# Routing search by counting: threshold masks as matmul weights and the experts' one-hot columns moving, in an attention, MoE and capacity-routing kernel

## The chip, the cores and the metric

The kernel runs on one core of one Trainium2 chip. The metric is the device time of one execution in microseconds (us); lower is better. Three runs of the kernel before took 1225.27, 1225.92 and 1227.36 us, the median is 1225.92 us.

## The reference, cut to what matters

Three stages, each feeding the next. The change touches mainly the third, the search for the routing's thresholds.

```python
# 1 attention of x (8,8,512,64) and state (8,8,32,64), both ways, concatenated: 8 x 544 tokens of 512
# 2 dense MoE on the tokens
h = x @ w_in                                            # 512 -> 2048
g = np.maximum(h, 0.0) + np.log1p(np.exp(-np.abs(h)))   # softplus
x = g @ w_out                                           # 2048 -> 512
# 3 routing with a capacity
N, E = x.shape[0], 8
cap = N // E
logits = x @ w_gate
for idx in np.argsort(-logits.flatten()):               # best pair first
    tok, e = idx // E, idx % E
    if assigned[tok] >= 0 or counts[e] >= cap:
        continue
    assigned[tok] = e
    counts[e] += 1
for e in range(E):
    mask = assigned == e
    out[mask] = np.maximum(x[mask] @ w1[e], 0.0) @ w2[e]
```

The program has 8 x 544 = 4352 tokens, and a capacity of 544 per expert.

## The kernel before, in words

**Stages.** Attention and the dense MoE are interleaved over eight batches of 544 tokens (`attention`, generator in batches 1 to 7, beside `mlp1`, the product with w_in at L485, the softplus at L520 to L550, and `mlp2`, the product with w_out at L569 to L580). Each fp32 operand is split in a high and a low part, and each product is three matmuls. The softplus is four steps: ACT copies p_h out (L520), takes an exponential and a logarithm (L527, L528, the helper `softplus_log`, one call of which does both for a pending tile), and DVE adds them up to g (L540). ACT then writes g_hi (L548), POOL the difference g_lo (L551). L540 also frees the PSUM bank of p_h, of which there are few, so that PE's next L485 waits for it. In `attention`, DVE scales and transposes Z into `back` (L290, L291), ACT copies that to at_hi (L292), and POOL takes at_lo.

**The routing.** The greedy loop of the reference is done in eight phases; each fills one expert. A phase finds, for all eight experts at once, the value v at which an expert becomes full, as the bits of a float, in seven steps (five bits in the first four, four bits in the last three: 31, 31, 31, 31, 15, 15 thresholds and 16, with one more column in the last). Tokens lie on 128 partitions by NJ = 34 columns, padded to NJ4 = 36. A step is:
- mask, L1015 on DVE: mk[token, threshold] = v >= threshold;
- count, L912 (`by_some`) on PE: the one-hot of each token's expert is the weight, the masks move, and the counts come out with a row per expert. `by_some` takes 2 columns of tokens per matmul in phase 0 (17 matmuls) and 4 in phases 1 to 6 (9 matmuls), each for another diagonal block of the result;
- sum of the blocks and comparison with the places that are left, L1036 to L1039 on DVE (8 rows of 31): pe, then sat;
- L1046 on PE: a matmul with ones brings the number of full experts of each threshold to all partitions;
- L1049 on DVE: d, df, the digit found, from which the next thresholds come (L1010).

After step 7 the phase ends with a tail: ohd, junk, cnt, s (L1054 to L1059) on 8 rows, T (L1062), one bf16 matmul that brings s to all partitions, gt, tie, cg, asg (L1065 to L1068), ec, em, ei (L1071 to L1073: which expert is filled), M (L1075, L1076), the matmul of M (L919), positions (L921 to L943), the matmuls with R (L912), the index list and a gather of the expert's tokens (xg).

**What sets the order.** `route` is a generator: at each `wait` it hands control back, and the code around it emits so many matmuls of the main work in between. Phase 0 runs between the last `mlp2` matmuls (717.9 to 756.6 us; fillers of 0.233 us each by a table BETWEEN), phases 1 to 6 between the expert matmuls (757 to 1061 us, slots AT1, AT2, AT3), one phase beside the previous expert; phase 7 has nothing to search. PE runs in program order, so a count whose mask isn't there yet stops the main work too; DVE, ACT, POOL and SP also run in program order. `route_consts` makes the search's constants, at step s == NFT + 4 of `mlp1` (DVE, 175.0 to 178.3 us). `y_state` writes the state tokens' result, four DMAs of 32 rows in each of two parts (L634), on the queues of SP and ACT in turn.

Of the kernel before, what the change touches and what calls it, by code (L numbers as in the profile page):

```python
# [22 lines left out]
NJ = N // 128  # L23
# [7 lines left out]
def attn_moe_kernel(ctx, tc, x_s, x_t, state_t, w_in, w_out, w_gate, w1, w2, out):  # L31
# [46 lines left out]
    iof = const.tile([8, 16], F32, name="iof")  # L78
    tri = const.tile([128, 128], BF, name="tri")
    code = const.tile([128, E], F32, name="code")  # L80
    code8 = const.tile([E, 1], F32, name="code8")
# [170 lines left out]
    def attention(b):  # L252
# [31 lines left out]
        for par in range(2):  # L284
# [6 lines left out]
            V.transpose(back[:, par], Z[:, par])  # L291
            A.activation(hi[:, par], back[:, par], AF.Copy)  # L292
# [368 lines left out]
    def first_step(j0, j1):  # L661
# [131 lines left out]
    for s in range(NX - 2):  # L793
        b, ft = divmod(s, NFT)
        if s == NX - NFT:
# [82 lines left out]
    iof_t, pel_t, rem8_t = small(1 << BITS[-1]), small((1 << BITS[-1]) + 1), small(1)  # L878
# [81 lines left out]
    def route(ph, slow=True):  # L960
# [31 lines left out]
        for s, bits in enumerate(BITS):  # L992
# [5 lines left out]
            if s or ph:  # L998
                mk = rt.tile([128, NJ, n + (2 if last else 0)], BF, name="mk", tag=f"mk{n}_{last}")
# [25 lines left out]
            ps = [p[0:E] for p in by_some(bg(), om, mk, w, 4 if slow else 2)]  # L1025
            sat = sats[n]
            pe = rt.tile([E, w], F32, name="pe", tag=f"pe{w}")
            if last:
                V.tensor_copy(pe, ps[0])
                for p in ps[1:-1]:  # L1030
                    V.tensor_tensor(pe, p, pe, op=OP.add)
                V.tensor_tensor(pel, ps[-1], pe, op=OP.add)
                pe = pel
                V.tensor_scalar(sat[0:E], pe[:, 1:1 + n], rem8, None, op0=OP.is_ge)
# [36 lines left out]
        V.tensor_tensor(ec, p[:, 0:E], code, op=OP.mult)  # L1071
# [300 lines left out]
```

## Time and profile before

| what | value |
|---|---|
| median of 3 runs | 1225.92 us |
| the profiled execution's own time | 1226.8 us |
| its span, first to last instruction | 1225.0 us |
| granted TensorE clock, mean | 0.990 |
| PE busy | 1159.3 us, 95% |
| DVE, ACT, POOL busy | 667.3, 639.2, 487.8 us |
| phase 0 of the search | 717.9 to 756.6 us |
| phases 1 to 6 | 770 to 1061 us |

The profile is of one execution. Its own time is 1.8 us more than its span, and 0.9 us more than the median of the runs. A row of the timeline is: start, duration, engine and line, operation, output<-inputs, shapes, count, and in brackets how long the engine sat idle before it and for whom. Matmuls are pipelined: the durations of neighbours overlap, and the distance from start to start is what one costs.

### The profile page before, as it was taken

The numbers are of one execution on the slowest core, as the hardware profiler recorded it, in microseconds if no ns is written. First come the engines' busy times: TensorE is split into PE (matmuls) and PEld (weight loads), VectorE is DVE, ScalarE is ACT, GpSimd is POOL, SyncE is SP. The second block draws the span as 40 slices with busy tenths as digits, with TensorE's granted clock in tenths as the row PEclk, the third lists the DMA queues.
The fourth block names the chain that finished last, engine by engine and source line by source line (L and its number), as shares of the span: only waits on it lengthen the run. The fifth ranks groups of instructions, "written<-read, shape, count | busy, mean of one in ns | idle before, by whom it ended". The sixth has DMA issues, their size and how long they took to land.

```text
span 1225.0 us, 21305 instructions
## 1 busy us (share of the span) xinstructions
PE 1159.3 (95%) x8291; PEld 910.3 (74%) x8291; DVE 667.3 (54%) x1797; ACT 639.2 (52%) x1277; POOL 487.8 (40%) x466
## 2 busy tenths in 40 slices
PE   4898999999999999999999997999999999999996
PEld 1565676777677776777677765879797988789895
DVE  6998545353363543634434266777685868751120
ACT  3776656666666666666666732533343333333330
POOL 0334323222232232222344425645647555546531
PEclk9998999999999999999999998999999999999999
DMA  7463021111201112002000003251523415234200
GB/s 241 139 202 127 1 70 35 53 52 36 69 1 52 52 35 58 13 36 69 1 18 18 1 18 123 88 194 40 180 92 129 150 68 172 104 108 140 89 18 37
DMA packets 51061, 95.78 MB, mean 78 GB/s; under 512 B 4624, under 2 KB 19088, under 8 KB 50960
## 3 DMA queue, kind: packets, MB, share of 16 engines
q1 hardware_dynamic: 45136, 76.33, 18.8%
q0 software_dynamic: 5632, 17.83, 4.2%
q8 instruction: 65, 1.06, 0.4%
q10 hardware_dynamic: 192, 0.26, 0.1%
q14 instruction: 36, 0.29, 0.1%
HBM read 76.58 MB, written 17.83 MB: 77 GB/s over the span
## 4 chain that ended last, share of the span: by engine, by line
PE 66%; DVE 17%; ACT 7%; issue 6%; POOL 2%; DMA 1%; SPq 0%; ACTq 0%; POOLq 0%; DVEq 0%
PE p_y L1310 12%; PE p_h L485 10%; PE p_y L1265 6%; PE p_y L569 6%; PE p_y L571 5%; PE p_h L1265 5%; PE p_y L573 5%; PE p_bg L912 2%; DVE g L540 2%; PE p_y L576 2%; PE p_bg L454 2%; PE p_bg L496 2%; PE p_y L578 2%; PE p_y L580 2%; PE p_h L1176 1%
## 5 line engine op out<-in xcount | busy, mean ns | idle before, releaser
L551 POOL TENSOR_TENSOR g_lo<-g,g_hi 128x512 fp32r<-128x512 f32 x127 | 164.9, 1299 | 340.7 <-ACT g_hi L548 327.3
L569 PE MATMUL p_y<-g_hi,wo_hi 128*128 128x512 f32 x448 | 185.0, 413 | 0.0
L571 PE MATMUL p_y<-g_hi,wo_lo 128*128 128x512 f32 x448 | 177.7, 397 | 3.7 <-POOL wo_lo L232 3.7
L573 PE MATMUL p_y<-g_lo,wo_hi 128*128 128x512 f32 x448 | 177.2, 396 | 0.0
L540 DVE SCALAR_TENSOR_TENSOR g<-p_h,t_sp 128x512 f32<-128x512 f32 x128 | 87.7, 686 | 122.7 <-ACT t_sp L528 121.8
L548 ACT ACTIVATE g_hi<-g 128x512 fp32r<-128x512 f32 x126 | 79.6, 632 | 124.0 <-DVE g L540 95.2
L569 PEld LDWEIGHTS p_y<-g_hi,wo_hi 128*128 128x128 f32 x448 | 85.1, 190 | 48.3 <-issue 15.9
L485 PE MATMUL p_h<-at_hi,P_hi 128*128 128x512 f32 x256 | 104.9, 410 | 8.1 <-DVE g L540 8.1
L1310 PE MATMUL p_y<-w2h,h2h 128*128 128x512 f32 x256 | 105.1, 411 | 0.0
L485 PE MATMUL p_h<-at_hi,P_lo 128*128 128x512 f32 x256 | 101.8, 398 | 0.0
L485 PE MATMUL p_h<-at_lo,P_hi 128*128 128x512 f32 x256 | 101.7, 397 | 0.0
L1310 PE MATMUL p_y<-w2l,h2h 128*128 128x512 f32 x256 | 101.5, 396 | 0.0
L1310 PE MATMUL p_y<-w2h,h2l 128*128 128x512 f32 x256 | 101.3, 396 | 0.0
L571 PEld LDWEIGHTS p_y<-g_hi,wo_lo 128*128 128x128 f32 x448 | 85.4, 191 | 21.0 <-POOL wo_lo L232 4.9
L573 PEld LDWEIGHTS p_y<-g_lo,wo_hi 128*128 128x128 f32 x448 | 85.2, 190 | 21.0 <-POOL g_lo L551 2.4
L1318 POOL DMA_INDIRECT out_dram<-ot,idx x40 | 39.4, 985 | 145.6 <-ACT ot L1316 68.9
L1149 POOL TENSOR_TENSOR w2l<-s2w,w2h 128x512 fp32r<-128x512 f32 x64 | 82.5, 1305 | 14.2 <-ACT w2h L1148 13.0
L520 ACT ACTIVATE t_sp<-p_h 128x512 f32<-128x512 f32 x128 | 75.3, 588 | 24.5 <-PE p_h L485 24.2
L1149 POOL TENSOR_TENSOR w1l<-s1w,w1h 128x512 fp32r<-128x512 f32 x63 | 80.4, 1300 | 11.2 <-ACT w1h L1148 10.3
L528 ACT ACTIVATE t_sp<-t_sp 128x512 f32<-128x512 f32 x128 | 80.9, 632 | 4.1
L527 ACT ACTIVATE t_sp<-t_sp 128x512 f32<-128x512 f32 x128 | 80.6, 630 | 2.0
L1265 PE MATMUL p_y<-yTh,w1h 128*128 128x288 f32 (+1 forms) x256 | 76.9, 300 | 0.6 <-DVE h2t L1274 0.6
(284 smaller groups left out, 2643.5 us busy)
## 6 DMA issues: line engine op xcount, KB each, us to landing
s1w<-in_moe_w_dram SPq DMA_DIRECT2D x8, 2048.0 KB, 8.4
s2w<-in_moe_w_dram SPq DMA_DIRECT2D x8, 2048.0 KB, 9.5
st<-in_moe_w_in_dram SPq DMA_DIRECT2D x16, 512.0 KB, 4.1
xT<-in_x_t_dram SPq DMA_DIRECT2D x16, 512.0 KB, 4.4
st<-in_moe_w_out_dram SPq DMA_DIRECT2D x16, 512.0 KB, 3.7
xt<-in_x_s_dram SPq DMA_DIRECT2D x8, 1024.0 KB, 5.8
y_d<-yz SPq DMA_DIRECT2D x48, 128.0 KB, 3.6
y_d<-s_g SPq DMA_DIRECT2D x8, 128.0 KB, 2.2
```

Of the source, the lines that this page charges most:

```text
L485: PE.matmul(h, l[:, f0:f0 + 128], r[:, par, :], start=(n == 0), stop=(n == 5))
L527: A.activation(t, t, AF.Exp, scale=-1.0)
L528: A.activation(t, t, AF.Ln, bias=1.0)
L540: V.scalar_tensor_tensor(g[:, :w], hps.pop(s)[:, :w], 0.0, tsp.pop(s)[:, :w], op0=OP.max, op1=OP.add)
L548: A.activation(hi[:, c], g[:, c], AF.Copy)
L551: (G if on[1] == "G" else V).tensor_tensor(lo[:, c], g[:, c], hi[:, c].bitcast(F32), op=OP.subtract)
L569: PE.matmul(yb[j], wo_hi[:, ft, c], hi, start=st, stop=False)
L571: PE.matmul(yb[j], wo_lo[:, ft, c], hi, start=False, stop=False)
L573: PE.matmul(yb[j], wo_hi[:, ft, c], lo, start=False, stop=sp)
L1149: eng.tensor_tensor(lo, src, hi.bitcast(F32), op=OP.subtract)
L1265: PE.matmul(p[:, :w], l[:, k, f], r[:, k, c], start=(n == 0), stop=(n == 11))
L1310: PE.matmul(p, l[:, ft, c], r[:, ft, :], start=(n == 0), stop=(n == 23))
```

## The change

- **Counting.** The mask tiles are now 32 wide per token column, zeroed once (`mks`, `first[3]`), of which 31, 15 or 17 are written. They are the weights (4 columns of tokens, 128 x 128), and the one-hot (now 8 wide, `ohu`) moves with 32 columns: 9 matmuls a step in every phase. Counts have a row per threshold and a column per expert.
- **The rest of the search in that layout.** pe and sat are [thresholds, 8]; each step adds four blocks, in phase 0 too, where there were two. L1046 becomes a matmul of a constant 128 x 128 (`taken`) with sat, 8 columns; df is one TENSOR_REDUCE.
- **The tail.** ohd, junk and cnt go; oh2 is one operation. T is two fp32 matmuls with 128 x 128 weights (oh2 spread out) and pel moving. s8 and rem8 are read from its result, and stand ahead of gt, tie, cg and asg.
- **Constants.** `route_consts` loses five small operations, and two of the memsets, and gains 20 (row23, and six for each of three `taken`).
- **Beside it.** `attention` calls `softplus_log()` ahead of the at_hi copy; `y_state` sends the first part's four DMAs from SP.

```diff
+        for n, t in taken.items():
+            k0, k1 = (1, 15) if n == 16 else (0, n - 1)
+            rows = tp.tile([128, 2], F32, name=f"rows{n}")
+            V.tensor_scalar(rows[:, 0:1], pf, float(k0), None, op0=OP.is_ge)
+            V.tensor_scalar(rows[:, 1:2], pf, float(k1), None, op0=OP.is_le)
+            V.tensor_tensor(rows[:, 0:1], rows[:, 0:1], rows[:, 1:2], op=OP.mult)
+            V.tensor_scalar(rows[:, 1:2], pf, 32.0, float(1 << 23), op0=OP.is_equal, op1=OP.mult)
+            V.tensor_tensor(rows[:, 0:1], rows[:, 0:1], rows[:, 1:2], op=OP.add)
+            V.tensor_copy(t, bc(rows[:, 0:1], [128, 128]))
...
             V.transpose(back[:, par], Z[:, par])
+            softplus_log()
             A.activation(hi[:, par], back[:, par], AF.Copy)
...
-            (SP if i % 2 else A).dma_start(y_d[r0:r0 + NS], t[i * NS:(i + 1) * NS, 0])
+            (A if j and i % 2 else SP).dma_start(y_d[r0:r0 + NS], t[i * NS:(i + 1) * NS, 0])
...
-                V.tensor_tensor(mk[:, :, 0:w], bc(v[:, :, None], [128, NJ, w]), bc(tf[:, None, :], [128, NJ, w]),
+                V.tensor_tensor(mk[:, 0:NJ, 0:w], bc(v[:, :, None], [128, NJ, w]), bc(tf[:, None, :], [128, NJ, w]),
                                 op=OP.is_ge)
...
-            ps = [p[0:E] for p in by_some(bg(), om, mk, w, 4 if slow else 2)]
+            p = bg()
+            for j in range(0, NJ4, 4):
+                PE.matmul(p[:, 0:4 * E], mk[:, j:j + 4].rearrange("p a b -> p (a b)"),
+                          om[:, j:j + 4].rearrange("p a b -> p (a b)"), start=(j == 0), stop=(j + 4 >= NJ4))
+            ps = [p[q * 32:q * 32 + w, q * E:(q + 1) * E] for q in range(4)]
...
-                V.tensor_scalar(pe, ps[-1], -1.0, rem8, op0=OP.mult, op1=OP.add)
+                V.scalar_tensor_tensor(pe, ps[3], -1.0, rem8[0:w], op0=OP.mult, op1=OP.add)
                 for p in ps[1:-1]:
                     V.scalar_tensor_tensor(pe, p, -1.0, pe, op0=OP.mult, op1=OP.add)
-                V.tensor_tensor(sat[0:E], ps[0], pe, op=OP.is_ge)
+                V.tensor_tensor(sat[0:w], ps[0], pe, op=OP.is_ge)
...
-            PE.matmul(q[:, 0:n], ones_b, sat, start=True, stop=True)
-            d16 = rt.tile([128, n], F32, name="d16", tag=f"d{n}")
+            PE.matmul(q[:, 0:E], taken[16 if last else n], sat, start=True, stop=True)
             df = rt.tile([128, 1], F32, name="df")
-            V.scalar_tensor_tensor(d16, q[:, 0:n], 0.5, one23[:, 0:n], op0=OP.is_ge, op1=OP.add, accum_out=df)
+            V.tensor_reduce(df, q[:, 0:E], axis=AX, op=OP.max)
...
-        ohd = rt.tile([E, n + 1], F32, name="ohd")
-        V.tensor_scalar(ohd, iof_t[:, 0:n + 1], df[0:E], None, op0=OP.is_equal)
-        cnt = rt.tile([E, 2], F32, name="cnt")
-        junk = rt.tile([E, n + 1], F32, name="junk")
-        for i in range(2):
-            V.scalar_tensor_tensor(junk, pe[:, i:i + n + 1], 1.0, ohd, op0=OP.mult, op1=OP.mult, accum_out=cnt[:, i:i + 1])
-        V.tensor_tensor(s8[0:E], cnt[:, 0:1], rem8, op=OP.is_ge)
+        oh2 = rt.tile([128, 2], F32, name="oh2")
+        V.tensor_scalar(oh2, row23p, df, None, op0=OP.is_equal)
         yield from wait(WT, slow)
         p = bg()
-        PE.matmul(p[:, 0:E], bc(s8, [128, 128]), i8b, start=True, stop=True)
-        V.tensor_tensor(rem8, rem8, cnt[:, 1:2], op=OP.subtract)
+        for i in range(2):
+            PE.matmul(p[:, i * E:(i + 1) * E], bc(oh2[:, i:i + 1], [128, 128]), pel, start=True, stop=True)
+        V.tensor_tensor(s8, p[:, 0:E], rem8, op=OP.is_ge)
+        V.tensor_tensor(rem8, rem8, p[:, E:2 * E], op=OP.subtract)
         tf = fb.bitcast(F32)
...
-        V.tensor_tensor(ec, p[:, 0:E], code, op=OP.mult)
+        V.tensor_tensor(ec, s8, code, op=OP.mult)
```

How this moves instructions, at three places. Line numbers of the changed program are higher by 5 to 13 from L110 on. The first is ACT in the middle of an attention batch of the program before (at_hi is the copy of the transposed attention, t_sp the pending softplus):

```order
L548 ACTIVATE g_hi<-g 128x512
L520 ACTIVATE t_sp<-p_h 128x512
L292 ACTIVATE at_hi<-back 128x512
L527 ACTIVATE t_sp<-t_sp 128x512
L528 ACTIVATE t_sp<-t_sp 128x512
```

and of the changed program:

```order
L554 ACTIVATE g_hi<-g 128x512
L526 ACTIVATE t_sp<-p_h 128x512
L533 ACTIVATE t_sp<-t_sp 128x512
L534 ACTIVATE t_sp<-t_sp 128x512
L298 ACTIVATE at_hi<-back 128x512
```

The exponential and the logarithm now stand ahead of the copy that waits for DVE's transpose; so at 12 places.

The second is DVE at the tail of phase 0, from the digit of the last step on (L1049, now L1065). T, the matmul, lies between s (L1059) and ec (L1071) before; in the changed program it lies between oh2 (L1070) and L1075 (s8):

```order
L1054 TENSOR_SCALAR ohd<-p_bg_6872,df 8x16
L1058 SCALAR_TENSOR_TENSOR junk,cnt<-p_bg_6872,ohd 8x16 x2
L1059 TENSOR_TENSOR s_6886<-cnt,p_bg_6872 8x1
L1063 TENSOR_TENSOR p_bg_6872<-p_bg_6872,cnt 8x1
L1065 TENSOR_SCALAR p_bg_6872<-v_5974,p_bg_6872 128x34
L1066 TENSOR_SCALAR p_bg_6872<-v_5974,p_bg_6872 128x34
L1067 TENSOR_TENSOR p_bg_6872<-cu_5975,p_bg_6872 128x34
L1068 TENSOR_TENSOR asg<-asg,p_bg_6872 128x34
L1071 TENSOR_TENSOR ec<-p_bg_7334,code 128x8
```

```order
L1070 TENSOR_SCALAR oh_7278<-p_bg_6890,df 128x2
L1075 TENSOR_TENSOR p_bg_6890<-p_bg_7302,rem_6895 128x8
L1076 TENSOR_TENSOR rem_6895<-rem_6895,p_bg_7302 128x8
L1078 TENSOR_SCALAR p_bg_6890<-v_5991,p_bg_6890 128x34
L1079 TENSOR_SCALAR p_bg_6890<-v_5991,p_bg_6890 128x34
L1080 TENSOR_TENSOR p_bg_6890<-cu_5992,p_bg_6890 128x34
L1081 TENSOR_TENSOR asg<-asg,p_bg_6890 128x34
L1084 TENSOR_TENSOR ec<-p_bg_6890,code 128x8
```

Before, the four operations on 34 columns stood ahead of the first reader of T's result; now they stand behind it.

The third is PE at the first count of phase 0. In the changed program (before: 17 pairs of `LDWEIGHTS ohu` and `MATMUL p_bg<-mk,ohu 64x62`):

```order
L582 MATMUL p_y_6041<-wo_hi,g_hi 128x512
L1041 LDWEIGHTS mk_5994
L1041 MATMUL p_bg_6934<-ohu_5993,mk_5994 128x32
L1041 LDWEIGHTS mk_5994
L1041 MATMUL p_bg_6934<-ohu_5993,mk_5994 128x32
```

Nine such pairs take the place of 17; the main work around them stands as before.

## Rows read from the trace of the kernel before

**Rows 1.** One of PE's waits: us in total, times, longest.

```profile
PE p_h L485 <- DVE g L540: 8.1, 12, 1.4
```

**Rows 2.** Timeline of PE, DVE and ACT at the attention copy of one batch.

```profile
279.33 0.39 PE L573 MATMUL p_y<-g_lo,wo_hi 128*128 128x512 f32 x1
280.57 0.50 PE L485 MATMUL p_h<-at_hi,P_hi 128*128 128x512 f32 x1 [0.85 <-DVE g L540]
...
279.82 0.69 DVE L540 SCALAR_TENSOR_TENSOR g<-p_h,t_sp 128x512 f32<-128x512 f32 x1 [1.95 <-ACT t_sp L528]
...
277.90 0.63 ACT L292 ACTIVATE at_hi<-back 128x512 fp32r<-128x512 f32 x1 [3.05 <-DVE back L291]
```

**Rows 3.** Timeline of PE and ACT at the first part of `y_state`.

```profile
745.16 0.49 PE L576 MATMUL p_y<-wo_hi,g_hi 128*128 128x512 f32 x1 [1.36 <-ACT g_hi L548]
...
744.79 0.51 ACT L548 ACTIVATE g_hi<-s_g 128x128 fp32r<-128x128 f32 x2 [3.06 <-DVE yt L631]
```

**Rows 4.** Timeline of PE at a count of phase 0, with the fillers around it.

```profile
717.57 0.40 PE L576 MATMUL p_y<-wo_hi,g_hi 128*128 128x512 f32 x1
717.89 0.72 PE L912 MATMUL p_bg<-mk,ohu 128*64 128x62 bf16 x17
...
718.88 0.40 PE L580 MATMUL p_y<-wo_hi,g_lo 128*128 128x512 f32 x1
```

**Rows 5.** Timeline of PE at a count over 31 thresholds of phase 1.

```profile
776.16 0.28 PE L1265 MATMUL p_h<-yTh,w1h 128*128 128x256 f32 x1
776.27 0.64 PE L912 MATMUL p_bg<-mk,ohu 128*128 128x124 bf16 x9
...
776.95 0.28 PE L1265 MATMUL p_h<-yTh,w1l 128*128 128x256 f32 x1
777.07 0.28 PE L1265 MATMUL p_h<-yTh,w1h 128*128 128x256 f32 x1
```

**Rows 6.** Timeline of PE at a count over 15 thresholds of phase 1.

```profile
787.57 0.29 PE L1265 MATMUL p_h<-yTh,w1h 128*128 128x288 f32 x1
787.71 0.42 PE L912 MATMUL p_bg<-mk,ohu 128*128 128x60 bf16 x9
...
788.19 0.29 PE L1265 MATMUL p_h<-yTh,w1l 128*128 128x288 f32 x1
788.32 0.29 PE L1265 MATMUL p_h<-yTh,w1h 128*128 128x288 f32 x1
```

**Rows 7.** Timeline of PE at four fp32 transposes with 128 x 128 weights.

```profile
778.98 0.60 PE L1176 MATMUL p_h<-ident,xg 128*128 128x128 f32 x4
```

**Rows 8.** Groups of DVE's instructions, 757 to 1084 us: busy us, mean ns, idle before.

```profile
L1015 DVE TENSOR_TENSOR mk<-v,p_bg 128x1054 bf16<-128x1054 f32 x18 | 22.5, 1252 | 0.6
L1038 DVE SCALAR_TENSOR_TENSOR pe<-p_bg,pe 8x31 f32<-8x31 f32 x48 | 8.8, 182 | 1.7
L1066 DVE TENSOR_SCALAR p_bg<-v,p_bg 128x34 f32<-128x34 f32 x6 | 1.6, 260 | 0.2
```

**Rows 9.** DVE's line for R, ns min/median/max; it writes 17 of every 34 elements.

```profile
L943 DVE TENSOR_TENSOR R<-a,dig x16: 747/759/3747, 754.8 to 1082.8; 128x578 bf16<-128x578 f32 x16
```

**Rows 10.** Timeline at the end of `route_consts`: DVE, then PE.

```profile
177.02 0.29 DVE L116 TENSOR_SCALAR tri<-io,pf 128x128 bf16<-128x128 int32 x1
177.59 0.16 DVE L121 TENSOR_SCALAR rid<-pq 128x1 int32<-128x1 int32 x1
178.33 0.68 DVE L540 SCALAR_TENSOR_TENSOR g<-p_h,t_sp 128x512 f32<-128x512 f32 x1
...
180.08 0.40 PE L485 MATMUL p_h<-at_hi,P_hi 128*128 128x512 f32 x1
```

**Rows 11.** Timeline at the tail of phase 0: T, the first reader of T, the matmul of M.

```profile
748.18 0.18 PE L1062 MATMUL p_bg<-i8b,s 128*128 128x8 bf16 x1
749.45 0.16 PE L919 MATMUL p_bg<-ones_b,M 128*68 128x1 bf16 x1
...
748.42 0.17 DVE L1071 TENSOR_TENSOR ec<-p_bg,code 128x8 f32<-128x8 f32 x1 [0.17 <-PE p_bg L1062]
```

More of the change, by code (lines that the diff above doesn't have):

```diff
@@ L77, in attn_moe_kernel @@
     io = const.tile([128, 128], I32, name="io")
-    iof = const.tile([8, 16], F32, name="iof")
+    row23 = const.tile([128, 2], F32, name="row23")
+    taken = {n: const.tile([128, 128], BF, name=f"taken{n}") for n in (31, 15, 16)}
     tri = const.tile([128, 128], BF, name="tri")
     code = const.tile([128, E], F32, name="code")
-    code8 = const.tile([E, 1], F32, name="code8")
     pat = const.tile([128, sum((1 << b) - 1 for b in BITS) + 1], I32, name="pat")
@@ L84, in attn_moe_kernel @@
     ones_b = const.tile([128, 128], BF, name="ones_b")
-    one23 = const.tile([128, 31], F32, name="one23")
-    i8b = const.tile([128, E], BF, name="i8b")
     dig = const.tile([128, 2, NJ], F32, name="dig")
@@ L112, in route_consts @@
         V.memset(ones_b, 1.0)
-        V.tensor_copy(i8b, ident[:, 0:8])
         pf = tp.tile([128, 1], F32, name="pf")
         V.tensor_copy(pf, pcol)
+        for i in range(2):
+            V.tensor_scalar(row23[:, i:i + 1], pf, float((1 << 23) - i), None, op0=OP.add)
+        for n, t in taken.items():
[7 more added lines that the diff above has]
+            V.tensor_copy(t, bc(rows[:, 0:1], [128, 128]))
         V.tensor_scalar(tri, io, pf, None, op0=OP.is_gt)
@@ L803, in attn_moe_kernel @@
             first += [sp_.tile([128, NJ], F32, name="v0"), sp_.tile([128, NJ], F32, name="cu0"),
-                      sp_.tile([128, NJ4, 32], BF, name="ohu0"), sp_.tile([128, NJ, (1 << BITS[0]) - 1], BF, name="mk0")]
+                      sp_.tile([128, NJ4, E], BF, name="ohu0"), sp_.tile([128, NJ4, 32], BF, name="mk0")]
             G.memset(first[2], 0.0)
+            G.memset(first[3], 0.0)
         if s == NFT:
@@ L877, in attn_moe_kernel @@
     est = small(E)
-    iof_t, pel_t, rem8_t = small(1 << BITS[-1]), small((1 << BITS[-1]) + 1), small(1)
     sl, sh = small(NJ, sci), small(NJ, sci)
@@ L881, in attn_moe_kernel @@
     thr_t, patfb_t = small(31, sci), small(31, sci)
-    iof_t, pel, rem8 = iof_t[0:E], pel_t[0:E], rem8_t[0:E]
-    V.tensor_copy(iof_t, iof)
+    s8, row23p = small(E), small(2)
+    V.tensor_copy(row23p, row23)
     V.memset(U, 1.0)
@@ L886, in attn_moe_kernel @@
     V.memset(asg, 0.0)
+    rem8 = rt.tile([128, E], F32, name="rem8")
     V.memset(rem8, float(CAP))
+    pel = rt.tile([128, E], F32, name="pel")
+    V.memset(pel, 0.0)
     opn = rt.tile([128, E], F32, name="opn")
     V.memset(opn, 1.0)
-    ohu = rt.tile([128, NJ4, 32], BF, name="ohu")
+    ohu = rt.tile([128, NJ4, E], BF, name="ohu")
     G.memset(ohu, 0.0)
+    mks = {n: rt.tile([128, NJ4, 32], BF, name=f"mk{n}") for n in (31, 15)}
     ohl = rt.tile([128, NJ4, 32], BF, name="ohl")
     G.memset(ohl[:, NJ:], 0.0)
-    sats = {n: rt.tile([128, n], BF, name=f"sat{n}") for n in sorted({(1 << b) - 1 for b in BITS})}
-    s8 = rt.tile([128, 1], BF, name="s8")
-    for t in (*sats.values(), s8):
+    sats = {n: rt.tile([128, E], BF, name=f"sat{n}") for n in (31, 15, 16)}
+    for t in sats.values():
+        G.memset(t, 0.0)
+        G.memset(t[32:33], 1.0)
+    for t in mks.values():
         G.memset(t, 0.0)
@@ L998, in route @@
             if s or ph:
-                mk = rt.tile([128, NJ, n + (2 if last else 0)], BF, name="mk", tag=f"mk{n}_{last}")
+                mk = mks[n]
             if s == 0:
@@ L1024, in route @@
             yield from wait(W31 if n > 15 else W15, slow)
-            ps = [p[0:E] for p in by_some(bg(), om, mk, w, 4 if slow else 2)]
-            sat = sats[n]
-            pe = rt.tile([E, w], F32, name="pe", tag=f"pe{w}")
+            p = bg()
[3 more added lines that the diff above has]
+            ps = [p[q * 32:q * 32 + w, q * E:(q + 1) * E] for q in range(4)]
+            sat = sats[16 if last else n]
+            pe = rt.tile([w, E], F32, name="pe", tag=f"pe{w}")
             if last:
                 V.tensor_copy(pe, ps[0])
[L1030 to L1034, printed above, removed]
+                V.tensor_tensor(pe, ps[1], pe, op=OP.add)
+                V.tensor_tensor(pe, ps[2], pe, op=OP.add)
+                V.tensor_tensor(pel[0:w], ps[3], pe, op=OP.add)
+                V.tensor_tensor(sat[0:w], pel[0:w], rem8[0:w], op=OP.is_ge)
             else:
-                V.tensor_scalar(pe, ps[-1], -1.0, rem8, op0=OP.mult, op1=OP.add)
+                V.scalar_tensor_tensor(pe, ps[3], -1.0, rem8[0:w], op0=OP.mult, op1=OP.add)
                 for p in ps[1:-1]:
                     V.scalar_tensor_tensor(pe, p, -1.0, pe, op0=OP.mult, op1=OP.add)
-                V.tensor_tensor(sat[0:E], ps[0], pe, op=OP.is_ge)
+                V.tensor_tensor(sat[0:w], ps[0], pe, op=OP.is_ge)
             if 0 < s and not last:
@@ L1081, in route @@
         V.scalar_tensor_tensor(U, v, tf, U, op0=OP.is_le, op1=OP.mult)
-        e8 = rt.tile([E, 1], F32, name="e8")
-        V.tensor_scalar(e8, code8, em[0:E], 1.0e6, op0=OP.is_equal, op1=OP.mult)
-        V.tensor_tensor(rem8, rem8, e8, op=OP.add)
         V.tensor_scalar(est, code, em, None, op0=OP.is_equal)
+        V.scalar_tensor_tensor(rem8, est, 1.0e6, rem8, op0=OP.mult, op1=OP.add)
         V.tensor_tensor(opn, opn, est, op=OP.subtract)
```

12 lines of the change are left out of this document (4 added, 8 removed).

## The prediction, made before the changed kernel had run

> **What bounds the kernel now.** I read the page's busy times first: PE is busy for 1159.3 of the 1225.0 us of the span, so what PE issues less, or waits less, is time won, and a faster DVE or ACT is worth something only where PE waits for it. Next PE's list of waits. One entry belongs to a place that the change touches: L485 waits 12 times, 8.1 us in all, for DVE's g [rows 1]. The timeline at one such place [rows 2] shows why: the copy at_hi sat at the head of ACT's queue for 3.05 us, waiting for DVE's transpose, and the exponential and the logarithm of a tile long there stood behind it; g waited 1.95 us for them, and PE for g. Third, the timeline at `y_state`: ACT waited 3.06 us for DVE's yt, because two DMAs that read yt stood in its queue, and PE waited 1.36 us for the g_hi behind them [rows 3]. Last, the counts. They aren't waits but work on PE, and their price is what they push the next fillers back.
>
> All sums are against the profiled execution, 1226.8 us by its own time; the median of the runs is 0.9 us lower, and the number at the end stands against the median.
>
> **Attention, -8.4 us.** Moved ahead of at_hi, the logarithms run in the time in which ACT idled. g can then follow the transpose on DVE at 277.87, when at_hi began [rows 2], in place of 279.82, 1.95 us earlier, and PE had lost only about 1.0 us. The wait is gone with 0.9 us to spare. Of the 12 waits one (the longest, 1.4 us, in the first batch, before this loop) stays; 11 go, 8.1 - 1.4 = 6.7 us by the modelled ends. From start to start it is more: 280.57 - 279.33 = 1.24 us, less the usual pitch of 0.233, is 1.01 where the wait reads 0.85, so 0.16 more each, 11 x 0.16 = 1.8. Together 8.4. What is late next: at_hi itself, 1.2 us later behind both logarithms only where the transposes come early, and no PE row waits for it. Bounds: -8.4 and -4 (half comes back as a wait for the same g behind DVE's transposes).
>
> **`y_state`, -1.5 us.** 1.36 by the row, plus the same 0.16 [rows 3]. SP issues four DMAs in place of two; nothing stood near it on SP there, so I cost that at nothing. What covers it is that SP's next job, a weight load, stands well behind; without that cover this load would start later by the issue of two DMAs.
>
> **The count on PE, -8.5 us.** Price of a chain: from the filler ahead of it to one behind, less the pitch of the fillers. In phase 0, 718.88 - 717.57 less two of 0.233 is 0.84 us [rows 4]. Over 31 thresholds in phases 1 to 6, 777.07 - 776.16 less three of 0.12 is 0.55 [rows 5]; over 15, 788.32 - 787.57 less three of 0.133 is 0.35 [rows 6]. The new chain is nine matmuls with 32 columns and 128 x 128 weights, which the trace doesn't have. Upper bound: the nine of 60 columns, 0.35. Lower bound: 124 to 60 columns saved 0.20, so another 28 fewer could save 0.09, 0.26. I take 0.35, because the floor seems reached: the chains of phase 0 cost 0.05 a matmul at half the columns of the 124. That gives 7 x (0.84 - 0.35) = 3.4 in phase 0, 24 x 0.20 = 4.8 for 31 thresholds, nothing for 12 chains of 15, and 6 x 0.05 for those of 17 (an estimate between the two rows): -8.5. With 0.26, 49 x 0.09 = 4.4 more.
>
> The Trainium skill's page "TensorE: Matmul & The Clock Gate", section "Wait — 56ns, not 53.3ns?", puts a floor of about 25 ns under the distance of two matmuls however few their columns. By it nine would go from 0.35 to some 0.31 us at best, and the sum would be 2 us lower; rows 6, at 0.35 for nine, agree that little is left.
>
> **T, +1.4 us.** One bf16 matmul becomes two in fp32 with weights that must be loaded. The nearest row is four fp32 matmuls in 0.60 us [rows 7], so two are 0.30, against 0.18 for T now [rows 11]. Bounds +0.1 and +0.4 each; I take 0.2, times 7.
>
> **DVE between count and sat, +1.5 us.** Phase 0 adds two operations a step, 0.18 and a gap of some 0.04 each [rows 8], 0.43 us; the reduce in place of d and its accumulator gives back about 0.2, but behind the other matmul. Phase 0's fillers between count and L1046 are as few as three, 0.7 us, and the count itself is 0.49 shorter, so PE comes sooner to a sat that is later. Where three to six fillers stand between, I get waits of 0.2 to 0.7 us in four steps, 1.5 in all. Bounds 0 and 3. Phases 1 to 6 had four blocks already; there I put 0.8 for waits at counts that are first in a phase, where the load of the mask as weight can't run ahead of the mask. Bounds 0 and 2.
>
> **The tail, +2.4 us.** Before, the four operations on 34 columns ran before T's result was there, and ec followed T by 0.24 us [rows 11]. Now s8, rem8 and these four stand between T and ec: at most 4 x 0.26 [rows 8], and 2 x 0.2 (small ones, [rows 8]), 1.4 us in all, while oh2 alone stands ahead of T in place of four operations. T itself can't come earlier, its place among the fillers is fixed. In phase 0, M's matmul came 1.27 us after T, now it has a path of some 2.5: wait 1.2. In phases 1 to 6 the slot from T to M is 2.2 us or more; there I work out 0.07 to 0.35 each, 1.2 in all. Bounds 0 and 4.
>
> **Constants, +1.9 us.** `route_consts` gains 20 operations on DVE and loses six. Those on one column take 0.16 and a gap of 0.03 [rows 10], five for each `taken`, and a cast of 128 x 128 like tri, 0.2 to 0.3: 3 x 1.0, two for row23 0.27, less 0.5: 2.75 us. The next thing in DVE's queue is g, at 178.33 for 0.68, and PE's L485 at 180.08 wants the bank that g frees: 1.07 us of slack [rows 10]. 2.75 - 1.07 = 1.7, and 0.2 for g_lo behind it. Bounds +0.5 and +2.5. The zeroing of more tiles on POOL (1.1 us where it was) ends before g_lo's input is there: nothing.
>
> **Sum.** -8.4 - 1.5 - 8.5 + 1.4 + 1.5 + 0.8 + 2.4 + 1.9 = -10.4 us. 1226.8 - 10.4 = 1216.4 for a profiled execution; against the median, **1215.5 us**.
>
> **Rivals.**
> 1. *The DVE stalls are hidden.* PE has slack that I counted as gone; the 4.7 us of DVE terms and half of T vanish, and the chain is at 0.3: -10.4 - 4.7 - 0.7 - 2.5 = -18, some 1208 us. For it: the slots of phases 1 to 6 are wide. Against: program order leaves T and M where they were. Chance 0.14.
> 2. *The attention wait moves.* g now comes right behind DVE's transpose, and the second wait of each batch may stay with other DVE work: -4 for -8.4, the time is 1220. For it: DVE is serial here. Against: 1.95 us gained on 1.0 lost [rows 2]. Chance 0.17.
> 3. *The search gets slower.* If the new DVE operations and the waits for weights cost 0.2 us in each of 42 steps, that takes 8.4 back: 1224, within what can be told from no change, which for this kernel is 0.2%, 2.5 us. For it: PE's lead shrinks at each step by what the chain gains. Against: before, just 7 counts waited for a mask. Chance 0.08.
> 4. *The load of mask weights isn't hidden* (slower). If each matmul had to wait for its own 128 columns of weights, it would cost what the fp32 ones do, 0.60 / 4 = 0.15 [rows 7], nine 1.35, and 49 chains 49 x 1.0 = 49 us more: 1215.5 + 49 = 1264. It turns the sign once a pair costs 10.4 / (49 x 9) = 0.024 us over 0.039. Against it: rows 6 are nine matmuls with nine different 128 x 128 bf16 weights in 0.35, 0.039 each. Masks written with gaps (31 of 32) could also be slow on DVE, but R, 17 of every 34, goes at the masks' own rate: 1252 - 759 ns for 1054 - 578 elements is 1.04 ns each [rows 8, 9]. Chance 0.05.
>
> The same page, section "LDWEIGHTS (loading the stationary operand)", gives a load of 128 columns about 107 ns, and its Part 2 says that loads are pulled ahead of running matmuls. Unhidden, a chain would be 0.96, and the time some 1245; rows 6 side with the pulling ahead.
>
> **How the numbers follow.** The forecast keeps 0.56. Its own bounds, taken together with about half of each end, are 1211 to 1220. The range of 8 in 10 takes in rival 2 and the nearer half of rival 1: 1209 to 1221.5. Faster by more than 0.2%: the forecast, rivals 1 and 2, and a part of rival 3, 0.89. Same: 0.06, from rival 3. Slower: 0.05, rival 4.
>
> **What would show it.** Right: PE's list of waits without L485 for g but in one place around 34 us and a new one near 180; no L576 for g_hi near 745; chains of phase 0 at 0.35 in place of 0.84, those over 31 thresholds at 0.35 for 0.55; a wait at the matmul of M in phase 0 and short ones in the other phases. Wrong: L485 still waiting in attention, masks of more than 1.3 us on DVE, chains above 0.5, or waits for sat or masks all over phases 1 to 6.

## The result, and the profile after

The changed kernel took 1216.05 us (median of 6 runs, 1214.23 to 1216.95); the kernel before, over the same runs, 1227.16. The ratio is 0.991, 95% interval 0.9897 to 0.9922: some 11 us faster. The profiled execution took 1215.9 us where the prediction's sum gave 1216.4. The sum is right; two of its groups of terms are wrong by 2 to 3 us each, and cancel.

From the page of the changed kernel, part 1, where PE was busy for 1159.3 us before:

```profile
PE 1152.4 (95%) x8256; PEld 906.2 (75%) x8256; DVE 661.1 (54%) x1742; ACT 640.9 (53%) x1277; POOL 489.6 (40%) x472
```

and from PE's list of waits (us in total, times, longest), which answers to [rows 1]:

```profile
PE p_bg L925 <- DVE R L956: 3.3, 3, 2.3
...
PE p_h L491 <- DVE g L546: 2.6, 2, 1.4
PE p_bg L1063 <- DVE sat L1051: 2.3, 2, 1.8
...
PE p_bg L1063 <- DVE sat L1056: 1.3, 3, 0.6
...
PE p_bg L932 <- DVE M L1089: 0.9, 1, 0.9
```

The wait of L491 (L485 before) for g has shrunk from 12 times to the two that the prediction named, near 34 and 182 us, and L576's for g_hi is gone. L1063, the matmul that takes sat, waits 2.3 us for L1051, the sat of step 7, which nobody had on the list; the wait for R (L912 before, L925 now), 1.9 us before, is 3.3.

Where the time went, by the start of the same matmul in both executions:

| up to | before | after | difference | part | forecast |
|---|---|---|---|---|---|
| L573, ahead of the constants | 174.91 | 175.50 | +0.6 | +0.6 | 0 |
| L569, behind them | 182.18 | 184.56 | +2.4 | +1.8 | +1.9 |
| first L576, ahead of phase 0 | 711.67 | 702.97 | -8.7 | -11.1 | -8.4 |
| R's chain of phase 0 | 756.60 | 745.67 | -10.9 | -2.2 | -2.0 |
| L1265 behind the last R | 1084.06 | 1073.17 | -10.9 | 0.0 | -1.9 |

The first line is scatter between executions of one kernel, as e8 and e11 will show. Phase 0's forecast is y_state, its counts, sat, T and tail, -1.5 - 3.4 + 1.5 + 0.2 + 1.2 = -2.0 (to a tenth); that of phases 1 to 7 the rest of the sum.

**Attention.** The place of [rows 2] in the timeline of the changed kernel, PE, then DVE, then ACT:

```profile
279.47 0.39 PE L579 MATMUL p_y<-g_lo,wo_hi 128*128 128x512 f32 x1
279.70 0.39 PE L491 MATMUL p_h<-at_hi,P_hi 128*128 128x512 f32 x1
...
277.31 0.65 DVE L546 SCALAR_TENSOR_TENSOR g<-p_h,t_sp 128x512 f32<-128x512 f32 x1
...
277.42 0.63 ACT L298 ACTIVATE at_hi<-back 128x512 fp32r<-128x512 f32 x1 [1.87 <-DVE back L296]
```

The distance from L573 to L485 is 0.23 in place of 1.24, and g ends 1.7 us ahead of PE.

**The counts.** A chain of phase 0 and one over 31 thresholds, with fillers, to hold against [rows 4] and [rows 5]:

```profile
708.86 0.40 PE L582 MATMUL p_y<-wo_hi,g_hi 128*128 128x512 f32 x1
709.10 0.39 PE L1041 MATMUL p_bg<-ohu,mk 128*128 128x32 bf16 x9
...
709.88 0.39 PE L582 MATMUL p_y<-wo_hi,g_hi 128*128 128x512 f32 x1
...
765.42 0.28 PE L1276 MATMUL p_h<-yTh,w1h 128*128 128x256 f32 x1
765.54 0.39 PE L1041 MATMUL p_bg<-ohu,mk 128*128 128x32 bf16 x9
...
765.98 0.28 PE L1276 MATMUL p_h<-yTh,w1l 128*128 128x256 f32 x1
```

709.88 - 708.86 less three pitches of 0.233 is 0.32 us, and 765.98 - 765.42 less two of 0.12 is 0.32: for 0.84 and 0.55 before.

**The new wait.** DVE's sat of step 7 and POOL at that moment, then PE, timeline of phase 5:

```profile
990.89 0.17 DVE L1050 TENSOR_TENSOR pel<-p_bg,pe 17x8 f32<-17x8 f32 x1
991.09 2.51 DVE L1051 TENSOR_TENSOR sat<-pel,rem 17x8 bf16<-17x8 f32 x1
...
991.08 2.49 POOL L1160 TENSOR_TENSOR w2l<-s2w,w2h 128x512 fp32r<-128x512 f32 x2
...
993.66 0.18 PE L1063 MATMUL p_bg<-sat,taken 128*128 128x8 bf16 x1 [1.81 <-DVE sat L1051]
```

An operation on 17 x 8 numbers took 2.51 us, and ended when POOL's two had ended. Nothing in its own work explains that. Both its inputs, pel and rem8, lie in SBUF since the change; before, `small` had put them in PSUM (the p_bg in L1034's input), and L1034 never took over 0.23 us.

**R and the clock.** Near 1060 us R was late beside two POOL operations as well, and PE waited 2.29 us. The windows of the changed kernel behind it (us; PE, PEld, DVE, ACT, POOL busy; granted clock as a share of full speed; DMA share; GB/s):

```profile
1058.50:1061.00 2.50, 1.05 (x13) 1.05 (x13) 2.50 (x6) 0.00 (x0) 0.78 (x1) 1.00 0.00 0
1061.00:1063.50 2.50, 2.20 (x12) 1.85 (x10) 2.22 (x15) 0.91 (x2) 0.68 (x1) 0.52 0.00 0
1063.50:1066.50 3.00, 3.00 (x23) 2.94 (x23) 1.66 (x10) 0.99 (x3) 2.21 (x3) 0.83 0.50 120
```

After a stretch in which PE was busy for 1.05 of 2.5 us, the granted clock is 0.52 over the next 2.5 us, nearly all of them at the lower of its two levels, 1.2 GHz, and 0.83 over the 3 us behind. By the starts of the same matmuls in both traces this costs 1.2 us on top of the wait.

### The profile page after: what moved, and what is told of

Its sections match the earlier page's. It is cut to its first block, busy times and chain, and to the rows that moved or that the text cites. A ratio compares the mean times of both kernels' runs of the same rounds, so it can differ in the third digit from the quotient of the medians.

```text
span 1214.1 us, 21167 instructions
## 1 busy us (share of the span) xinstructions
PE 1152.4 (95%) x8256; PEld 906.2 (75%) x8256; DVE 661.1 (54%) x1742; ACT 640.9 (53%) x1277; POOL 489.6 (40%) x472
## 4 chain that ended last, share of the span: by engine, by line
PE 76%; DVE 12%; issue 6%; POOL 2%; DMA 1%; ACT 1%; SPq 0%; POOLq 0%; DVEq 0%; ACTq 0%
PE p_h L491 13%; PE p_y L1321 12%; PE p_y L575 8%; PE p_y L577 8%; PE p_y L579 7%; PE p_y L1276 6%; PE p_h L1276 5%; PE p_bg L460 2%; PE p_y L582 2%; PE p_y L586 2%; PE p_bg L502 2%; PE p_y L584 2%; PE p_h L1187 1%; DVE c_a L198 1%; DMA st<-in_moe_w_in_dram 1%
## 5 line engine op out<-in xcount | busy, mean ns | idle before, releaser
L579 PE MATMUL p_y<-g_lo,wo_hi 128*128 128x512 f32 x448 | 177.5, 396 | 0.0
L491 PE MATMUL p_h<-at_hi,P_hi 128*128 128x512 f32 x256 | 103.7, 405 | 2.7 <-DVE g L546 2.6
L491 PE MATMUL p_h<-at_hi,P_lo 128*128 128x512 f32 x256 | 101.7, 397 | 0.0
L491 PE MATMUL p_h<-at_lo,P_hi 128*128 128x512 f32 x256 | 101.5, 397 | 0.0
L579 PEld LDWEIGHTS p_y<-g_lo,wo_hi 128*128 128x128 f32 x448 | 85.2, 190 | 20.1 <-POOL g_lo L557 0.9
L1276 PE MATMUL p_y<-yTl,w1h 128*128 128x288 f32 (+1 forms) x256 | 78.2, 305 | 0.0
```

The costliest lines, as they stand in the source:

```text
L491: PE.matmul(h, l[:, f0:f0 + 128], r[:, par, :], start=(n == 0), stop=(n == 5))
L579: PE.matmul(yb[j], wo_hi[:, ft, c], lo, start=False, stop=sp)
L1276: PE.matmul(p[:, :w], l[:, k, f], r[:, k, c], start=(n == 0), stop=(n == 11))
```

## The experiments

Theory A is what the two traces say: attention gave 11 us, and the new search, whose counts save what was forecast and more, gives it back by waits. Theory B is the prediction's sum as it stood. Each kernel ran in 4 or 5 rounds beside the kernel before; "before" moves by 3 us from session to session, so ratios to it are compared across sessions.

### e1: the logarithms alone

```diff
             V.transpose(back[:, par], Z[:, par])
+            softplus_log()
             A.activation(hi[:, par], back[:, par], AF.Copy)
```

> The kernel before with the one line that moves the logarithms ahead of the at_hi copy, nothing else. Theory A (read from the two traces: a stall of PE for g costs more than its own length, because the matmul after it, g_lo's matmul and one later wait are late too): 11 us faster than before. Theory B (the prediction's term, the stalls alone): 8.4 us faster. Rival (the wait moves to DVE's transposes): 4 us faster.

Measured: 1215.95 against 1226.95 us, ratio 0.9905 (0.9890 to 0.9921), 11.0 us faster. Theory A holds and the rival falls; B's 8.4 us would be a ratio of 0.9932, outside the interval. One line is as fast as the whole change.

### e2: both lines beside the search

```diff
+            softplus_log()
...
-            (SP if i % 2 else A).dma_start(y_d[r0:r0 + NS], t[i * NS:(i + 1) * NS, 0])
+            (A if j and i % 2 else SP).dma_start(y_d[r0:r0 + NS], t[i * NS:(i + 1) * NS, 0])
```

> The kernel before with the moved logarithms and the four DMAs of y_state on SP, and the search as it was. Theory A: attention 11.0 and y_state 1.7, so 12.7 us faster than before, some 1.5 us faster than the whole change, because the new search is a net loss. Theory B: 8.4 + 1.5 = 9.9 us faster than before, and the whole change 0.5 us faster than this.

Measured: 1213.35 us, ratio 0.9887 (0.9871 to 0.9902), 13.6 us faster, against 0.991 for the whole change. So the new search, as submitted, costs 2.7 us on top of them, though the two intervals just touch. In e2's profile y_state's wait is gone, worth 1.6 us by the L576 behind it, and the stretch of attention is 12.1 us shorter than before (more on that under the prediction): 13.7 together.

### e3: the search alone

The changed kernel with these two lines put back.

> The changed kernel with the logarithms and the y_state DMAs put back to where they were, so only the search, its tail and its constants are new. Theory A (constants +1.8, phase 0 -0.5, phases 1 to 7 about 0): 1 to 2 us slower than before. Theory B (the prediction's sum for these terms): 0.5 us faster than before.

Measured: 1232.87 us, ratio 1.0039 (1.0026 to 1.0053), 5.9 us slower, more than A had said. The sign is A's. The size has a second cause, the clock; the windows of e3 over the tail of phase 0:

```profile
743.00:747.00 4.00, 2.41 (x18) 1.47 (x17) 1.95 (x9) 0.67 (x3) 0.94 (x3) 1.00 0.08 19
747.00:750.00 3.00, 2.82 (x8) 2.15 (x9) 0.55 (x3) 0.94 (x4) 1.34 (x3) 0.62 0.26 68
750.00:753.00 3.00, 3.00 (x14) 2.45 (x14) 0.63 (x4) 0.62 (x2) 1.38 (x3) 0.81 0.00 0
```

y_state's wait is back, 1.77 us long here for 1.36 in [rows 3], and behind it the clock falls to 0.62, where before it stayed at 1.00 over the same place. The stretch from y_state to M lost 3.0 us against before, and 1.3 in the changed kernel. It fell once more behind the wait for sat of step 7 near 1010 us, to 0.51 over 3.5 us, and 1.4 us were lost there that the changed kernel, with the same wait, didn't lose. The profiled execution is the slowest of e3's five (granted clock 0.982); the others had 0.985, and before had 0.987 to 0.990 beside them. The side lines and the search aren't independent: 5.9 without them, 2.7 with them.

### e4: sat against the constant 0

```diff
-                V.tensor_copy(pe, ps[0])
+                V.scalar_tensor_tensor(pe, ps[0], -1.0, rem8[0:w], op0=OP.mult, op1=OP.add)
...
-                V.tensor_tensor(pel[0:w], ps[3], pe, op=OP.add)
-                V.tensor_tensor(sat[0:w], pel[0:w], rem8[0:w], op=OP.is_ge)
+                V.tensor_tensor(pel[0:w], ps[3], pe, op=OP.subtract)
+                V.tensor_scalar(sat[0:w], pel[0:w], 0.0, None, op0=OP.is_ge)
```

> The changed kernel with the places that are left subtracted in the first of the four sums of step 7, so that sat is a comparison with the constant 0 and has one SBUF input in place of two; s8 and rem8 follow from the difference. As many operations on DVE. Theory A (sat in step 7, 0.15 us otherwise, took 2.51 and 1.27 us in two phases because both its inputs lie in SBUF and POOL was at a long operation on two SBUF inputs): no sat above 0.3 us, PE's two waits for L1051 (2.3 us) gone, 2 to 2.5 us faster than the changed kernel. Rival (DVE was held up by something else at that moment): the delay stays or moves to a neighbour, no difference.

Measured: 1215.65 us, ratio 0.9901 (0.9886 to 0.9916), no difference, and the wait is there as it was (timeline of e4, DVE and POOL):

```profile
991.27 2.52 DVE L1051 TENSOR_SCALAR sat<-pel 17x8 bf16<-17x8 f32 x1
...
991.26 2.49 POOL L1160 TENSOR_TENSOR w2l<-s2w,w2h 128x512 fp32r<-128x512 f32 x2
```

A miss: two SBUF inputs are not needed; one, with no PSUM input beside it, waits as well. The theory was mended to "reads SBUF alone".

### e5: sat from PSUM

```diff
-                V.tensor_tensor(pel[0:w], ps[3], pe, op=OP.subtract)
-                V.tensor_scalar(sat[0:w], pel[0:w], 0.0, None, op0=OP.is_ge)
+                V.tensor_tensor(sat[0:w], ps[3], pe, op=OP.is_ge)
+                V.tensor_tensor(pel[0:w], ps[3], pe, op=OP.subtract)
```

(against e4)

> The changed kernel, with sat of step 7 read from the count's last block in PSUM and the sums in SBUF (as in the other six steps), and pel worked out behind it. As many operations. Theory A, mended (a DVE operation that reads SBUF alone waits while POOL works on two SBUF tensors; one that reads a PSUM operand doesn't): no sat above 0.3 us, PE's two waits of 2.3 us for it gone, 1.5 to 3 us faster than the changed kernel (1213 to 1214.5). Rival (DVE waits for POOL whatever it reads): the 2.5 us stay.

Measured: 1212.71 us, ratio 0.9884 (0.9869 to 0.9900), 3.3 us faster than the changed kernel; by the same matmuls in both traces 2.6 of it lie at the two sats of step 7. Sat's lines, ns min/median/max, in e5, and in the changed kernel that of step 7 and that of the six other steps:

```profile
L1050 DVE TENSOR_TENSOR sat<-p_bg,pe x7: 167/168/169, 732.5 to 1041.0; 17x8 bf16<-17x8 f32 x7
```

```profile
L1051 DVE TENSOR_TENSOR sat<-pel,rem x7: 153/154/2511, 732.5 to 1045.1; 17x8 bf16<-17x8 f32 x7
L1056 DVE TENSOR_TENSOR sat<-p_bg,pe x42: 153/154/155, 710.2 to 1040.3; 31x8 bf16<-31x8 f32 x28, 15x8 bf16<-15x8 f32 x14
```

In e5 sat stands one operation earlier, and at phase 5 is done just before POOL begins, so that place alone proves little. The third row does: of these 42 sats, with one input in PSUM, 21 began while POOL was inside such an operation, and the longest took 0.155 us. Of the three of L1051 that met POOL, two waited to its end; the third began in the same instant as POOL's and didn't. The kernel before settles it for step 7 itself: there sat reads PSUM, and in phases 4 and 5 it began inside such a POOL operation and took what it takes everywhere (timeline of before, DVE and POOL):

```profile
952.14 0.23 DVE L1034 TENSOR_SCALAR sat<-p_bg 8x15 bf16<-8x15 f32 x1
...
952.01 1.29 POOL L1149 TENSOR_TENSOR w2l<-s2w,w2h 128x512 fp32r<-128x512 f32 x1
```

"Reads SBUF alone" is too wide, though. In the same trace three operations that read and write SBUF alone fell into one POOL operation; the reduction (ec and em are in SBUF) and the one on a single column took what they take elsewhere, and only M, 0.23 us otherwise, waited to POOL's end:

```profile
956.14 0.16 DVE L1072 TENSOR_REDUCE em<-ec 128x1 f32<-128x8 f32 x1
956.34 0.15 DVE L1073 TENSOR_SCALAR ei<-em 128x1 int32<-128x1 f32 x1
956.41 0.44 DVE L1075 TENSOR_SCALAR M<-asg,em 128x34 bf16<-128x34 f32 x1
...
955.52 1.29 POOL L1149 TENSOR_TENSOR w2l<-s2w,w2h 128x512 fp32r<-128x512 f32 x1 [0.24 <-ACT w2h L1148]
```

So of the operations that read SBUF alone some wait and some don't. In the changed kernel all those that read a tensor in PSUM went on inside POOL's operations; where only the scalar operand lay there (L1031, whose tensor v is in SBUF) one took 1.30 us for 0.31.

The Trainium skill, page "SBUF — State Buffer", section "Who interferes with whom", draws the line more finely: DVE and POOL share one pair of SBUF ports, a DVE operation with two SBUF inputs contends with a POOL operation that reads SBUF, `copy`, `cast` and `tensor_scalar` can as well in their 2-port modes, and one with at most one SBUF input outside these modes doesn't. The changed kernel, e4 and e5 agree with the three cases, 2.51, 2.52 and 0.17 us; that e4's operation ran in such a mode no profile here shows.

### e6: the tail's order

```diff
-        V.tensor_tensor(s8, p[:, 0:E], rem8, op=OP.is_ge)
-        V.tensor_tensor(rem8, rem8, p[:, E:2 * E], op=OP.subtract)
...
         V.tensor_tensor(asg, asg, cg, op=OP.add)
+        V.tensor_tensor(s8, p[:, 0:E], rem8, op=OP.is_ge)
...
         V.scalar_tensor_tensor(M2[:, NJ:], cu, em, tie, op0=OP.is_equal, op1=OP.mult)
+        V.tensor_tensor(rem8, rem8, p[:, E:2 * E], op=OP.subtract)
```

> The changed kernel with s8 moved behind gt, tie, cg and asg, and rem8 behind M, as the order was before. The prediction's term for the tail: 1.2 us of waits at the matmul of M in phase 0 and 1.2 in the six others; of these the moved operations are 1.1 us of DVE per phase. If the term holds: M's wait in phase 0 gone, 1.5 to 2.4 us faster than the changed kernel. Rival (the fillers hide it, and what the trace shows in phases 1 to 6 is the two fp32 matmuls): 1.0 us faster, from phase 0 alone.

Measured: 1214.78 us, ratio 0.9897 (0.9882 to 0.9912), 1.3 us faster by the medians, and the intervals overlap. The trace says more, again by the same matmul in both: M of phase 0 comes 0.9 us sooner, and those of phases 1 to 6 gain 0.1 to 0.3 each, 1.0 together. That is 1.9, the term and not the rival. It doesn't all arrive: behind the wait for sat near 993 us, which e6 still has, the clock fell in e6 (1.4 us lost) and R near 1060 met POOL otherwise (0.8 won).

### e7: constants on POOL

The three blocks on `taken` with `G.` for `V.`.

> The changed kernel with the three blocks that make the constant weights of the digit's matmul (18 operations) on POOL in place of DVE. If the prediction's term holds (+1.9 us, by DVE's queue ahead of g): the wait of L491 for g near 182 us gone, 1.5 to 2 us faster than the changed kernel. Rival (POOL is late for g_lo instead): 0 to 1 us.

Measured: 1214.62 us, ratio 0.9901 (0.9886 to 0.9916), 1.4 us faster by the medians, between the term and the rival, and the intervals overlap. From its PE timeline:

```profile
180.25 0.39 PE L491 MATMUL p_h<-at_hi,P_hi 128*128 128x512 f32 x1
...
183.10 0.50 PE L579 MATMUL p_y<-g_lo,wo_hi 128*128 128x512 f32 x1 [0.83 <-POOL g_lo L557]
```

L491 came 1.85 us sooner than the 182.10 of the changed kernel, but the L579 ahead of it had come 0.44 sooner already (180.02 for 180.46). So 1.4 us were gained, and then g_lo, behind the constants in POOL's queue, took 0.7 back. The 0.7 that are left are the rival's; in e8's trace it is 0.5.

### e8, e10, e11: all repairs, with and without R's constant in PSUM

```diff
+    V.tensor_copy(digp, dig)
...
-            V.tensor_tensor(R[:, :, d * 17:(d + 1) * 17], a17, bc(dig[:, d, :, None], [128, NJ, 17]), op=OP.mult)
+            V.tensor_tensor(R[:, :, d * 17:(d + 1) * 17], a17, bc(digp[:, d, :, None], [128, NJ, 17]), op=OP.mult)
```

(digp is a `small` tile, in PSUM; e5, e6 and e7 are in it too)

> The changed kernel with e5, e6 and e7 together, and the constant of R's product (dig) copied to PSUM, so that R doesn't read SBUF alone either. Theory A: 2.3 (sat) + 1.5 to 2.4 (tail) + 1.8 (constants) + 2 to 4 (R's two waits of 2.3 and 0.9 us, and the lower granted clock behind them) = 7.5 to 10 us faster than the changed kernel, 1206 to 1208.5, and 5 to 7 faster than e2. Rival (the waits come back elsewhere): 1210 to 1213, no better than e2 by 1 us or more.

Measured: 1207.12 us, ratio 0.9842 (0.9828 to 0.9855), 8.9 us faster than the changed kernel: theory A's total, with less from the constants than it put there (e7). R's line in e8 and in e10:

```profile
L957 DVE TENSOR_TENSOR R<-a,p_bg x16: 745/750/762, 742.0 to 1061.7; 128x578 bf16<-128x578 f32 x16
```

```profile
L956 DVE TENSOR_TENSOR R<-a,dig x16: 747/760/3746, 739.9 to 1064.0; 128x578 bf16<-128x578 f32 x16
```

> e8 with R's constant back in SBUF: the repairs of sat, tail and constants alone, beside e8 and e9 on the same chip. Theory A (R's wait of 2.3 us for POOL and the clock behind it): 2 to 4 us slower than e8. Rival (with the other repairs the timing is another and R meets POOL nowhere): same as e8 within 1 us.

Measured: 1208.92 us, ratio 0.9854, against e11's 1207.36 on the same chip: 1.6 us, between theory and rival. R still waits up to 3 us in e10, but PE waits 1.6 us for it and not 3.3, and behind its longest wait, 1.4 us near 1064 us, the granted clock stayed at 1.00.

> e8 once more, on the chip of e10 and e12: 1206 to 1209, ratio to before 0.983 to 0.986.

Measured: 1207.36 us, ratio 0.9839 (0.9825 to 0.9852), as expected. e8 and e11 are one kernel; their first 60 us differ in the granted clock, 0.97 and 0.94 (rows of e8, then e11), as executions do whatever the kernel:

```profile
0.00:60.00 60.00, 36.34 (x275) 22.58 (x276) 48.14 (x92) 33.12 (x61) 11.23 (x14) 0.97 0.57 194
```

```profile
0.00:60.00 60.00, 39.05 (x272) 24.02 (x273) 48.27 (x94) 32.92 (x61) 11.53 (x14) 0.94 0.57 194
```

### e9, e12: the old search with the side lines and R's constant in PSUM

> e2 (the kernel before with both side lines, old search) and R's constant in PSUM as in e8. It has all of e8 but the new counting and its repairs. Theory A (the counts save 8.5 us on PE by the traces, T costs 2.0 of them, and repaired, little else): e9 is 4 to 6 us slower than e8, 1211 to 1213, and up to 2 faster than e2. Rival (the gain of e8 over e2 is mostly R's): within 1.5 us of e8.

Measured: 1213.25 us, ratio 0.9871 (0.9852 to 0.9890), level with e2 by medians. By ratios it is 3.6 us slower than e8, by medians 6.1, so it ran again beside e11.

> e9 once more, beside e11, because before ran 3 us slower beside e9 than beside e8: if the repaired counting is worth what the medians say, 5 to 6 us slower than e11; if what the ratios say, 3 to 4.

Measured: 1211.89 us, ratio 0.9878 (0.9863 to 0.9894), against 0.9839 on the same chip: 4.5 us by the medians, 4.8 by the ratios. The new counting is worth that much once repaired by e5, e6 and e7; as submitted, it was a loss of 2.7.

## Why the prediction was right, and where it was not

The time, the sign and most mechanisms held, yet the sum came out by two errors that cancel, and that they cancel is luck.

- **Attention, -8.4, measured -11.1 in the changed kernel's trace, -11.0 by the medians of e1.** The mechanism was right; the term was too small, because only the 11 stalls were counted. In the trace of before, what follows a stall is late as well:

```profile
280.57 0.50 PE L485 MATMUL p_h<-at_hi,P_hi 128*128 128x512 f32 x1 [0.85 <-DVE g L540]
280.90 0.40 PE L485 MATMUL p_h<-at_lo,P_hi 128*128 128x512 f32 x1
...
282.30 0.40 PE L571 MATMUL p_y<-g_hi,wo_lo 128*128 128x512 f32 x1
282.70 0.50 PE L573 MATMUL p_y<-g_lo,wo_hi 128*128 128x512 f32 x1
...
218.20 1.06 PE L308 MATMUL p_bg<-ident,ST 128*128 128x128 f32 x8 [0.87 <-DVE P_lo L462]
```

  The first matmul after a stall has 0.33 to the next, not 0.233: 0.1 each, 1.1 in all. g_lo is late behind the late g: 0.40 for 0.23, and 0.1 again behind it, five times, 1.4. One wait of 0.87 at 218 us hung on it too, 1.0. With 8.4 that is 11.9, and this is what the moved line gives where the search is the old one: from the L573 ahead of the first stall (208.81 us before) to the table's first L576 it is 502.86 us before, 490.78 in e1 and 490.79 in e2, 12.1 less. (e1's execution had lost 1.5 us ahead of that stretch, in its first 60 us.) In the changed kernel it is 491.73. The 0.95 between lie in steps under 0.03 us all over the stretch, in every kernel with the new search and in none with the old one; e3, with the new search alone, is 0.64 longer there than before. So the new search also makes the main matmuls ahead of it a little slower, and why is open.
- **y_state, -1.5:** -1.6, as worked out. **Constants, +1.9:** +1.8. The parts that the prediction lists for one `taken` add up to 1.2 us, not to the 1.0 of its sum; in the trace one takes 0.95 (L115 at 177.18 and again at 178.13 us).
- **Counts, -8.5:** the chain is 0.32 in all phases; I took the upper bound of 0.35. 7 x 0.52 in phase 0 is 3.6. In the other phases each count over 31 thresholds gave 0.24, over 15 0.03, over 17 0.05: 24 x 0.24 + 12 x 0.03 + 6 x 0.05 = 6.4. Together -10.0. The floor is there: inside the new chain the matmuls start 0.025 us apart, inside that of rows 6 0.026 to 0.031, so that the 28 columns fewer gave 0.03 a chain, as the 0.31 that the prediction set beside its own figure had it. The 0.05 of rows 4 was no floor.
- **T, +1.4:** it cost 0.3 us more, not 0.2, 0.43 in phase 1, and 2.35 in all. The price came from rows 7, where an fp32 transpose is one record of 0.11 us; each of T's two fp32 matmuls is two:

```profile
735.62 0.51 PE L1074 MATMUL p_bg<-pel,oh 128*128 128x8 f32 x4
```

- **Between count and sat, +1.5 for phase 0:** 1.4, by delays of 0.6, 0.2 and 0.2 at L1063 and of 0.4 at an L582 that waits for DVE's yt. **This is also the step that failed**, for step 7: it counted DVE's operations and not where their inputs lie. pel and rem8 moved from PSUM to SBUF, sat met POOL, and 0.6 and 1.9 us were lost in two phases. e5 took them back. The whole diff shows it (`small` against `rt.tile`); it should have been a rival.
- **First counts of a phase, +0.8:** nothing. PE's waits for the first mask of phases 2 to 6 are 0.33, 0.31, 0.78, 0.30 and 0.63 us before and 0.33, 0.34, 0.78, 0.30 and 0.64 after. That of phase 1 is 0.7 us longer, but with that phase's first two counts done the difference has moved by 0.2 only.
- **The tail, +2.4:** 1.9 by the trace of e6, 0.9 in phase 0 and 1.0 in the six others; the mechanism was right, both parts a little cheaper than worked out.
- **Phases 1 to 7 in sum,** by the starts of the same matmuls before and after: counts -6.4, T +2.0, sat of step 7 +2.6, the matmul of M +0.8, R's wait near 1060 us +2.1 and the lower clock behind it +1.2. Against them stand -1.3 because two waits for h2 just ahead of that R (0.57 and 0.27 us before) are gone, and -1.2 because phase 7's matmul of M and the last R wait less. With +0.4 from all the rest that is +0.2, and 0.0 was measured.
- **What the new search cost as submitted,** 2.7 us by e2, is 2.2 in the traces: constants +1.8, the slower matmuls ahead +0.95, phase 0 without y_state -0.6, phases 1 to 7 0.0.
- **Rivals.** Rival 3, a search that gets slower, is nearest to what became of phases 1 to 7, by another mechanism than it gave. Rival 4 didn't happen: nine mask weights take 0.32 us, and masks with gaps 1.255 us where they took 1.252. Rival 2 didn't happen. Rival 1's 1208 us is about where e8 lies, once the waits are taken out by hand.

## What to carry to other kernels

Read where an operand lies before costing an operation: a tiny DVE operation that reads SBUF alone can stand for the length of POOL's (not each one does), and a PSUM copy of one constant or sum removed that here. A stall costs more than its wait: the restart, what hangs on the late result, and, where PE was idle for long, the clock behind it. And take a change apart even when its total comes out as forecast: here one line beside the headline gave all of the gain, and the headline was a loss until three small repairs made it worth 4.5 us; with R's constant in PSUM as the fourth the kernel takes 1207 in place of 1216.

## What the runs showed of the hardware that was not expected

- DVE's sat of step 7 with inputs in SBUF took 2.51 and 2.52 us beside two POOL operations (the changed kernel, e4); with an input in PSUM no sat of any kernel took over 0.23. R, 578 elements, took 3.00 to 3.77 us at the worst in the ten kernels with both inputs in SBUF, and never over 0.762 in the four with one in PSUM. A reduction of eight SBUF elements took its usual 0.16 us inside a POOL operation.
- Nine bf16 matmuls, each with new 128 x 128 weights, start 0.025 us apart at 32 columns and 0.053 to 0.064 at 124; a plain fp32 matmul of 8 columns stands in the trace as two records, 0.11 us apart.
- The first fp32r matmul after a wait of about 1 us was followed after 0.33 in place of 0.233 us, at a granted clock of 1.00.
- After a wait of 2.3 us on PE in the midst of the kernel the granted clock was 0.52 over 2.5 us; behind one of 1.77 us in e3 it was 0.62, and behind that of 1.36 us at the same place before, 1.00. Behind the 1.8 us for sat of phase 5 it fell to 0.61 in e6 and 0.51 in e3, and stayed at 1.00 in the changed kernel: the length of the wait alone doesn't decide it, and what does was not tried.
